# Elementwise products of the GLU tiles on VectorE instead of GpSimd, in a fixed order, and earlier loads before the first tile

## The chip, the cores and the metric

The kernel runs on one core of a Trainium2 chip. The metric is device time in microseconds from the first to the last instruction of that core. Three runs of the kernel before took 3117.59, 3122.15 and 3123.36 us; the median, 3122.15 us, is the time before. The profiled execution has a span of 3119.8 us and a mean granted TensorE clock of 0.989.

## The reference

One block of a conditioned transformer and its gradients, for 2048 rows of 512 features in bfloat16. Cut to what matters:

```
mod = (silu(c) @ w_mod) -> sa, ca, ga, sb, cb, gb          # six rows of 512
h   = layernorm(x) * (1 + ca) + sa
x1  = x + ga * A(h)            # recurrent attention, 64 segments of 32 rows, 8 memory rows
h2  = layernorm(x1) * (1 + cb) + sb
g, u = h2 @ w_gate, h2 @ w_up                             # 512 -> 1792
hh  = sigmoid(g) * u
out = x1 + gb * (hh @ w_down)                              # 1792 -> 512
```

The kernel returns `out` and the gradients of a given `grad_out` (called `dout`) with respect to x, the memory, the weights, c and w_mod. For the part that the change touches these are, per row: `db = dout * gb`, `du = (db @ w_down^T) * sigmoid(g)`, `dg = du * (u - hh)`, the gradient through the second layernorm `dx1`, then `da = dx1 * ga` and the product `dx1 * A(h)` that is summed over rows into the gradient of ga.

## The kernel before

The work runs in five stages, one after the other: the forward recurrence over 64 segments (`phase2`), the GLU with its forward and its backward (`phase3`, first part), the weight gradients of the GLU (second part), the backward recurrence (`phase4`) and the weight gradients of the attention (`phase5`). The change touches the last segment of `phase2` (the seam) and the first part of `phase3`.

**The GLU pipeline.** The 2048 rows are 16 tiles of 128. `run_pipeline` runs seven stages s0 to s6 over them: in iteration `it`, tile `it - k` is in stage k, and the deepest stage is written first. s0 makes `x1`, the layernorm and `h2`, and `db`. s1 sends `h2` and `db` through two transposing DMAs into `hdT`. s2 makes gate and up products (8 groups of four matmuls, 448 columns wide), ScalarE takes the sigmoid `sg` and copies `u`; then come `hh` and `umh = u - hh`. s3 makes four groups of matmuls `dp`, each turned into a piece of `du` by VectorE (L1077), then `dg`. s4 makes the output product, which ScalarE evacuates as `b_bf` (L1096), and leaves `t1` and `o_sb` for later. s5 makes the gradient product `hp`; VectorE works on it in the chain `dxh`, `pr_cb`, `junk`, `bb`, `cc`, `ta`, and with ScalarE's `tb` (L1140) makes `dx1`. s6 sums four products over the rows with matmuls onto `acc_ps` and transposes `da`.

**PSUM.** All products of s2 to s5 go through five buffers (`psM`, `mm()`), used in turn: 14 per iteration. A group of matmuls can start only when the product five places before it has been evacuated.

**Who does the elementwise work.** VectorE does most of it. GpSimd does five operations per tile: `rstd` (a power of 128x1), `db` (L1013), `umh` (L1054), `o_sb` (L1102) and `pr_ga` (L1152, `pr3` in the code). GpSimd's queue also issues the row stores to DRAM.

**Order.** `pin(i0, engines)` ties each instruction of an engine to the one before it in the program, so that the engine runs them in the order in which they are written. Where an engine is not pinned, the framework's scheduler picks the order when the kernel is built. In `phase3` TensorE and ScalarE are pinned up to iteration 2 only, and VectorE is not pinned. `late` is a list of small functions put off to the next `flush()`, of which there is one in s3 (between the `du` and `dg`) and one after each iteration.

**The seam.** `phase2` is pinned on all engines. In the last segment (s == 63) the weights and rows of the GLU are loaded into the space of `Wv`, `Wk` and `Wq`, the attention weights, as these are used for the last time. GpSimd's queue issues `w_gate`, `w_up`, `w_down` (1792 KB each, L819 to L821) after the segment's two Vst copies. The sync queue issues, in this order, the segment's k and q rows (`late_rows`), the rows of tile 0 (`glu_load`, L925 to L928) and the four modulation rows spread over 128 partitions (`mod_bc`, L366, 256 KB each). Then tile 1's rows follow, and the stores of the last segment. `norm` (L883) is the previous segment's GpSimd product, which is put off to the start of a segment.

Of the kernel before, what the change touches and what calls it, by code (L numbers as in the profile page):

```python
# [40 lines left out]
class K:  # L41
# [392 lines left out]
    def phase2(self):  # L434
# [13 lines left out]
        with ExitStack() as ctx:  # L448
# [232 lines left out]
            for s in range(NS):  # L681
# [10 lines left out]
                def proj(x, hf, eng):  # L692
                    pass_half(x, hf, lambda c: hT[:, c, :], RA[x], eng)
                    if hf == 1 and x != "v" and s < NS - 1:
                        rows_out(RA[x], DR[x], s, 1)
# [78 lines left out]
                        self.pair_mm(ps, [OT[:, off(h):off(h) + 32] for h in hs], [Wo[:, h, :] for h in hs], n, H // 2)  # L774
                    return ps

                if norms:
                    norms.pop()()
                proj("k", 0, "dve")
                proj("k", 1, "act")  # L780
                if s == 0:
                    for f in firsts["k"]:
                        f()
# [15 lines left out]
                if s + 1 < NS:  # L799
                    v_tails(s + 1)  # L800
                if s == NS - 1:
                    late_rows()
                    self.glu_first = {0: self.glu_load(0, nc.sync)}
                    for i in (2, 4, 3, 5):
                        self.mod_bc(None, i, "", t=self.bcs[i])
                st_exp(0)
                st_exp(1)
                vshift()
# [7 lines left out]
                if s < NS - 1:  # L816
                    nc.sync.dma_start(Pst[:], ET[:, :], transpose=True)
                else:
                    nc.gpsimd.dma_start(self.w_gate, io["B_w_gate"].rearrange("(c p) f -> p c f", p=128))  # L819
                    nc.gpsimd.dma_start(self.w_up, io["B_w_up"].rearrange("(c p) f -> p c f", p=128))  # L820
                    nc.gpsimd.dma_start(self.w_down, io["B_w_down"].rearrange("(fc p) d -> p fc d", p=128))  # L821
                den(1, or2)
# [108 lines left out]
    def phase3(self):  # L931
# [9 lines left out]
        with ExitStack() as ctx:  # L941
# [52 lines left out]
            def s0(j):  # L994
                r0, r1 = j * 128, (j + 1) * 128
                load(j + 1)
                st = ins.pop(j)
                a_rows = st["a_rows"]
                t0 = sbp.tile([128, D], F32, name="t0", tag="f32tmp", bufs=5)
                nc.vector.tensor_tensor(t0[:], a_rows[:], ga_bc[:], op=ALU.mult)  # L1000
                x1 = sbp.tile([128, D], F32, name="x1", bufs=4)
                nc.vector.tensor_tensor(x1[:], t0[:], st["x0"][:], op=ALU.add)
                sts = sbp.tile([128, 6], F32, name="st", bufs=2)
                nc.vector.bn_stats(sts[:], x1[:])
                mv = sbp.tile([128, 2], F32, name="mv", bufs=2)
# [5 lines left out]
                nc.gpsimd.tensor_tensor(rstd[:], ve[:], mhalf[:], op=ALU.pow)  # L1011
                db = sbp.tile([128, D], BF16, name="db", bufs=2)
                nc.gpsimd.tensor_tensor(db[:], st["dout"][:], gb_bc[:], op=ALU.mult)  # L1013
                self.pin(i0, [mybir.EngineType.Pool])
                nc.gpsimd.dma_start(self.DBROWS[r0:r1, :], db[:])
                xh2 = sbp.tile([128, D], BF16, name="xh2", bufs=5)
                xhf = sbp.tile([128, D], F32, name="xhf", tag="f32tmp", bufs=5)
                nc.vector.tensor_scalar(xhf[:], x1[:], mv[:, 0:1], rstd[:, 0:1], op0=ALU.subtract, op1=ALU.mult)
                nc.scalar.activation(xh2[:], xhf[:], AF.Copy)
                h2a = sbp.tile([128, D], F32, name="h2a", tag="f32tmp", bufs=5)  # L1020
                nc.vector.tensor_tensor(h2a[:], xhf[:], cb1_bc[:], op=ALU.mult)
                h2 = sbp.tile([128, D], BF16, name="h2", bufs=2)
                nc.vector.tensor_tensor(h2[:], h2a[:], sb_bc[:], op=ALU.add)
                nc.gpsimd.dma_start(self.H2ROWS[r0:r1, :], h2[:])
                st.update(db=db, x1=x1, rstd=rstd, xh2=xh2, h2=h2)
                return st

            def s1(j, st):
                hdT = sbp.tile([128, 2 * DC, 128], BF16, name="hdT", bufs=2)
                nc.sync.dma_start(hdT[:, 0:DC, :], st["h2"][:], transpose=True)  # L1030
                nc.sync.dma_start(hdT[:, DC:2 * DC, :], st["db"][:], transpose=True)
                st["hdT"] = hdT
                return st

            def s2(j, st):
                r0, r1 = j * 128, (j + 1) * 128
                hdT = st["hdT"]
                sg = sbp.tile([128, F], BF16, name="sg", bufs=2)
                u = sbp.tile([128, F], BF16, name="u", bufs=1)
                hh = sbp.tile([128, F], BF16, name="hh", bufs=2)  # L1040
                umh = sbp.tile([128, F], BF16, name="umh", bufs=1)
                for ch in range(NCH):
                    sl = slice(ch * CH, (ch + 1) * CH)
                    gp = mm()
                    for c in range(DC):
                        nc.tensor.matmul(gp[:, 0:CH], lhsT=hdT[:, c, :], rhs=w_gate[:, c, sl], start=(c == 0), stop=(c == DC - 1))
                    nc.scalar.activation(sg[:, sl], gp[:, 0:CH], AF.Sigmoid)
                    up = mm()
                    for c in range(DC):
                        nc.tensor.matmul(up[:, 0:CH], lhsT=hdT[:, c, :], rhs=w_up[:, c, sl], start=(c == 0), stop=(c == DC - 1))  # L1050
                    self.evac("act", u[:, sl], up[:, 0:CH])
                nc.vector.tensor_tensor(hh[:], sg[:], u[:], op=ALU.mult)
                nc.gpsimd.dma_start(self.HHROWS[r0:r1, :], hh[:])
                nc.gpsimd.tensor_tensor(umh[:], u[:], hh[:], op=ALU.subtract)  # L1054
                st.update(sg=sg, hh=hh, umh=umh)
                return st

            late = []

            def flush():  # L1060
                while late:
                    late.pop(0)()

            def s3(j, st):
                r0, r1 = j * 128, (j + 1) * 128
# [19 lines left out]
            def s4(j, st):  # L1085
                r0, r1 = j * 128, (j + 1) * 128
                hhT = st["hhT"]
                bp = mm()
                for fc in range(FC):
                    nc.tensor.matmul(bp[:], lhsT=hhT[:, fc, :], rhs=w_down[:, fc, :], start=(fc == 0), stop=(fc == FC - 1))  # L1090
                duT = sbp.tile([128, FC, 128], BF16, name="duT", bufs=1)
                dgT = sbp.tile([128, FC, 128], BF16, name="dgT", bufs=1)
                nc.sync.dma_start(duT[:], st["du"][:], transpose=True)
                nc.sync.dma_start(dgT[:], st["dg"][:], transpose=True)
                b_bf = sbp.tile([128, D], BF16, name="b_bf", bufs=2)
                nc.scalar.activation(b_bf[:], bp[:], AF.Copy)  # L1096

                def out():
                    t1 = sbp.tile([128, D], F32, name="t1", tag="f32tmp", bufs=5)
                    nc.vector.tensor_tensor(t1[:], b_bf[:], gb_bc[:], op=ALU.mult)  # L1100
                    o_sb = sbp.tile([128, D], BF16, name="o_sb", bufs=2)
                    nc.gpsimd.tensor_tensor(o_sb[:], t1[:], st["x1"][:], op=ALU.add)  # L1102
                    nc.gpsimd.dma_start(out_rows[r0:r1, :], o_sb[:])

                late.append(out)
                st.update(duT=duT, dgT=dgT, b_bf=b_bf)
                return st

            def s5(j, st):
# [36 lines left out]
                def out():  # L1146
                    nc.vector.tensor_tensor(da[:], dx1[:], ga_bc[:], op=ALU.mult)
                    nc.gpsimd.dma_start(self.DAROWS[r0:r1, :], da[:])

                late.append(out)  # L1150
                pr3 = sbp.tile([128, D], BF16, name="pr_ga", bufs=1)
                nc.gpsimd.tensor_tensor(pr3[:], dx1[:], a_rows[:], op=ALU.mult)  # L1152
                st.update(dh2b=dh2b, pr2=pr2, pr3=pr3, da=da, pr=pr)
                return st

# [52 lines left out]
            later = after  # L1208

            def after(it):  # L1210
                flush()
                later(it)

            self.run_pipeline(NT, [s0, s1, s2, s3, s4, s5, s6], deepest_first=True, after=after)
            self.pin_behind(i0, self.pinned, [ET.PE, ET.DVE, ET.Activation, ET.Pool, ET.SP])
            accs = self.flat(self.Wk, 2 * DC * F, 2 * D, F32)
            nc.vector.tensor_copy(accs[:], acc_ps[:, :])
# [910 lines left out]
```

The softmax here doesn't subtract the row's maximum and nothing guards it: scores larger than these inputs give would overflow.

## Time and profile before

| Stretch of the span, us | Stage | What TensorE does |
|---|---|---|
| 0 to 1000 | forward recurrence | busy, paced by itself |
| 1001.9 to 1008.9 | transposes of w_gate | slowed by ScalarE's evacuations |
| 1008.9 to 1023.9 | seam | idle, 15.0 us |
| 1023.9 to 1075.4 | first GLU iterations, with transposes of w_down and w_up | 48.6 of 51.5 us busy |
| 1075.4 to 1319.7 | 12 regular iterations of 20.42 us (one longer) | 229.3 of 244.3 us busy |
| 1319.7 to 1376 | last iterations, mixed with weight gradients | 50.0 of 56.4 us busy |
| 1376 to 3119.8 | weight gradients, backward recurrence | busy |

How to read it: the profile gives a busy time for each engine in any stretch, and for each instruction the idle time of its engine just ahead of it, with the work that ended that idle time. Where TensorE has the largest share, only idle time of TensorE can be won back; what the other engines wait for matters only if it makes TensorE wait later.

### The profile page before, as it was taken

The numbers are of one execution on the slowest core, as the hardware profiler recorded it, in microseconds if no ns is written. First come the engines' busy times: TensorE is split into PE (matmuls) and PEld (weight loads), VectorE is DVE, ScalarE is ACT, GpSimd is POOL, SyncE is SP. The second block draws the span as 40 slices with busy tenths as digits, with TensorE's granted clock in tenths as the row PEclk, the third lists the DMA queues.
The fourth block names the chain that finished last, engine by engine and source line by source line (L and its number), as shares of the span: only waits on it lengthen the run. The fifth ranks groups of instructions, "written<-read, shape, count | busy, mean of one in ns | idle before, by whom it ended". The sixth has DMA issues, their size and how long they took to land.

```text
span 3119.8 us, 106172 instructions
## 1 busy us (share of the span) xinstructions
PE 3005.8 (96%) x43845; PEld 1837.6 (59%) x43845; DVE 1644.2 (53%) x3735; ACT 1266.7 (41%) x3056; POOL 1502.8 (48%) x3022
## 2 busy tenths in 40 slices
PE   6999999999998899989989999999999999999999
PEld 3666666666665444445567777777777754455454
DVE  5556556656655789842255555555655542322321
ACT  2555555555554433322155555555555530110111
POOL 3667766767665566621244444444444422333321
PEclk8999999999999999999999999999999999999999
DMA  9887788788788789897589999999999998666674
GB/s 298 215 215 201 208 214 207 204 207 214 205 205 251 187 211 209 202 280 252 187 220 242 239 250 242 245 244 247 241 239 246 244 267 287 203 199 214 198 236 145
DMA packets 845944, 703.54 MB, mean 226 GB/s; under 512 B 544306, under 2 KB 717906, under 8 KB 845076
## 3 DMA queue, kind: packets, MB, share of 16 engines
q1 hardware_dynamic: 714148, 486.69, 61.7%
q0 software_dynamic: 60656, 148.64, 14.7%
q10 hardware_dynamic: 70656, 61.41, 6.3%
q8 instruction: 345, 5.65, 0.8%
q14 instruction: 139, 1.14, 0.1%
HBM read 294.93 MB, written 276.35 MB: 183 GB/s over the span
## 4 chain that ended last, share of the span: by engine, by line
PE 50%; issue 3%; DMA 3%; POOL 1%; DVE 0%; SPq 0%; ACT 0%; POOLq 0%; ACTq 0%; DVEq 0%
PE gps L1918 9%; PE dh_ps L215 8%; PE g_ps L1580 6%; PE pass_ps L255 5%; PE gps5o L1932 4%; PE dhq_ps L223 4%; PE gps L1267 3%; PE dh_tps L215 3%; PE dp_ps L1559 2%; PE tps L1492 2%; PE dp_ps L1567 1%; PE turn_ps L1446 1%; PE dh_ft L320 1%; POOL out_dram L1922 1%; PE wtp L1333 1%
## 5 line engine op out<-in xcount | busy, mean ns | idle before, releaser
L1918 PE MATMUL gps<-rows,hrows 128*128 128x512 bf16 (+2 forms) x2160 | 417.5, 356 | 0.0
L1918 PEld LDWEIGHTS <-hrows 128*128 128x128 bf16 x2160 | 211.0, 98 | 204.8
L255 PEld LDWEIGHTS <-hT 128*32 128x32 bf16 x6144 | 158.7, 97 | 160.9 <-issue 1.9
L1624 POOL COPY dOst<-RAd 96x512 bf16<-96x512 bf16 x128 | 75.6, 612 | 312.7 <-DVE RAd L63 312.2
L1922 POOL DMA_DIRECT2D out_dram<-ot x108 | 81.3, 753 | 247.6 <-DVE ot L63 140.3
L63 DVE CAST ot<-gps 128x512 bf16<-128x512 f32 (+3 forms) x76 | 48.1, 633 | 273.7 <-PE gps L1918 186.8
L61 ACT ACTIVATE ot<-gps 128x512 bf16<-128x512 f32 (+3 forms) x75 | 41.3, 551 | 352.3 <-PE gps L1918 232.9
L883 POOL TENSOR_TENSOR Pst<-Pst,rden 120x1408 bf16<-120x1408 bf16 x63 | 159.5, 2532 | 44.8 <-issue 28.6
L61 ACT ACTIVATE dVT<-g_ps 128x512 bf16<-128x512 f32 (+1 forms) x192 | 109.4, 570 | 95.6 <-PE g_ps L1580 95.0
L63 DVE CAST RA0v<-pass_ps 128x512 bf16<-128x512 f32 x128 | 88.5, 692 | 89.4 <-PE pass_ps L255 86.9
L215 PE MATMUL dh_ps<-WvT,dVT 128*32 128x512 bf16 x2048 | 133.3, 380 | 0.0
L255 PE MATMUL pass_ps<-Wv,hT 128*32 128x512 bf16 x2048 | 133.3, 380 | 0.0
L1932 PE MATMUL gps5o<-WoT,rows 128*128 128x512 bf16 x592 | 128.3, 379 | 2.1 <-DMA rows<-OSR 2.1
L255 PE MATMUL pass_ps<-Wk,hT 128*32 128x512 bf16 x2048 | 123.3, 383 | 1.5 <-ACT hT L873 1.1
L1569 DVE SCALAR_TENSOR_TENSOR dS<-dp_ps,Pst_l 128x512 bf16<-128x512 f32 (+1 forms) x192 | 112.1, 640 | 22.7 <-PE dp_ps L1567 22.7
L223 PE MATMUL at_ps<-Wo,OT 128*32 128x256 bf16 x4096 | 123.5, 273 | 0.1
L255 PE MATMUL pass_ps<-WoT,dyT 128*32 128x256 bf16 (+1 forms) x3072 | 122.4, 308 | 0.9 <-ACT dyT L1698 0.9
L223 PE MATMUL dhq_ps<-WqT,dQT 128*32 128x256 bf16 x4096 | 122.9, 273 | 0.0
L215 PE MATMUL dh_ps<-WkT,dKT 128*32 128x512 bf16 x2048 | 122.3, 381 | 0.0
L255 PE MATMUL pass_ps<-Wq,hT 128*32 128x512 bf16 x2048 | 121.6, 379 | 0.0
L223 PEld LDWEIGHTS <-dQT 128*32 128x32 bf16 x4096 | 109.9, 97 | 15.5
L717 ACT ACTIVATE ET<-st_ps 128x480 bf16<-128x480 f32 (+1 forms) x192 | 96.0, 535 | 42.6 <-ACT qT L61 34.7
(419 smaller groups left out, 7228.2 us busy)
## 6 DMA issues: line engine op xcount, KB each, us to landing
OSR<-Ost SPq DMA_DIRECT2D x64, 352.0 KB
OT<-OT SPq DMA_DIRECT2D x64, 352.0 KB
VT<-VTr SPq DMA_DIRECT2D x64, 352.0 KB
PS<-Pst SPq DMA_DIRECT2D x64, 352.0 KB
OT_l<-OT SPq DMA_DIRECT2D x64, 352.0 KB
Pst_l<-PS SPq DMA_DIRECT2D x64, 352.0 KB
VT_l<-VT SPq DMA_DIRECT2D x64, 352.0 KB
DVR<-rows_x POOLq DMA_DIRECT2D x64, 352.0 KB
```

Of the source, the lines that this page charges most:

```text
L61: return nc.scalar.activation(out, in_, AF.Copy)
L63: return nc.vector.tensor_copy(out, in_)
L215: self.nc.tensor.matmul(ps[32 * j:32 * j + 32, :], lhsT=lhsT, rhs=w, start=(n < 4), stop=(n >= total - 4), tile_position=(0, 32 * j))
L223: nc.tensor.matmul(ps[32 * j:32 * j + 32, :], lhsT=x[k], rhs=w[k][:, 256 * d:256 * d + 256], start=(n == 0), stop=(n == total - 1), tile_p ...
L255: self.nc.tensor.matmul(ps[32 * j:32 * j + 32, :], lhsT=lhs(c), rhs=rhs, start=(c == 0), stop=(c == DC - 1), tile_position=(0, 32 * j))
L717: nc.scalar.activation(part3(ET, pi)[:, 0:n, 0:120], st_ps[:, 0:n, 0:120], AF.Exp, scale=cfg.scale)
L883: nc.gpsimd.tensor_tensor(Pst[0:120, :, :], Pst[0:120, :, :], rden[:, :].unsqueeze(2).to_broadcast([120, G, 128]), op=ALU.mult)
L1569: nc.vector.scalar_tensor_tensor(out=part3(dS, pi), in0=ps[:, 0:n, :], scalar=cfg.scale, in1=part3(Pst, pi), op0=ALU.mult, op1=ALU.mult)
L1580: nc.tensor.matmul(ps[:, j, :], lhsT=lh[:, g * GW:(g + 1) * GW], rhs=rh[:, g * GW:(g + 1) * GW], start=True, stop=True)
L1918: nc.tensor.matmul(ps[:, 0:ng * E], lhsT=hrows[:, tp_, c * 128:(c + 1) * 128], rhs=rows[:, tp_, 0:ng * E], start=(tp_ == 0), stop=(tp_ == ...
L1922: nc.gpsimd.dma_start(outw[c * 128:(c + 1) * 128, h0:h0 + 3 * (ng - 1) + 1:3, :], ot[:, 0:ng * E].rearrange("p (h e) -> p h e", e=E))
L1932: nc.tensor.matmul(pss[gg][:], lhsT=src[0][:, src[1], gg * E:(gg + 1) * E], rhs=dyrows[:, tp_, :], start=(tp_ == order[0]), stop=(tp_ == o ...
```

## The change

The stated aim is to take the tile products off GpSimd, to give VectorE an order in which the pieces of `du` come first, and to have the loads ahead of the first tile issued sooner. It has six edits:

1. `db`, `umh`, `o_sb` and `pr_ga` move from GpSimd to VectorE. `rstd` and the DMA issues stay on GpSimd.
2. `db` is made after `h2` in s0, no longer before it.
3. `hh`, its store and `umh` are put off (`late`) to the flush after the iteration; `pr_ga` is put off together with `da`.
4. The flush after an iteration comes before the other work of that place from iteration 5 on, and after it (the weight transposes of iterations 2 to 4) before that.
5. VectorE is pinned to program order in the whole GLU pipeline.
6. In the last segment of the recurrence `w_gate` is issued right after the k projection and ahead of `norm`; the modulation rows come first on the sync queue, then tile 0's rows, then the k and q rows.

```diff
-                if norms:
+                if s < NS - 1 and norms:
                     norms.pop()()
                 proj("k", 0, "dve")
                 proj("k", 1, "act")
+                if s == NS - 1:
+                    nc.gpsimd.dma_start(self.w_gate, io["B_w_gate"].rearrange("(c p) f -> p c f", p=128))
+                    norms.pop()()
...
                 if s == NS - 1:
-                    late_rows()
-                    self.glu_first = {0: self.glu_load(0, nc.sync)}
                     for i in (2, 4, 3, 5):
                         self.mod_bc(None, i, "", t=self.bcs[i])
+                    self.glu_first = {0: self.glu_load(0, nc.sync)}
+                    late_rows()
...
-                    nc.gpsimd.dma_start(self.w_gate, io["B_w_gate"].rearrange("(c p) f -> p c f", p=128))
                     nc.gpsimd.dma_start(self.w_up, io["B_w_up"].rearrange("(c p) f -> p c f", p=128))
...
-                db = sbp.tile([128, D], BF16, name="db", bufs=2)
-                nc.gpsimd.tensor_tensor(db[:], st["dout"][:], gb_bc[:], op=ALU.mult)
                 self.pin(i0, [mybir.EngineType.Pool])
-                nc.gpsimd.dma_start(self.DBROWS[r0:r1, :], db[:])
...
                 nc.gpsimd.dma_start(self.H2ROWS[r0:r1, :], h2[:])
+                db = sbp.tile([128, D], BF16, name="db", bufs=2)
+                nc.vector.tensor_tensor(db[:], st["dout"][:], gb_bc[:], op=ALU.mult)
+                nc.gpsimd.dma_start(self.DBROWS[r0:r1, :], db[:])
...
-                nc.vector.tensor_tensor(hh[:], sg[:], u[:], op=ALU.mult)
-                nc.gpsimd.dma_start(self.HHROWS[r0:r1, :], hh[:])
-                nc.gpsimd.tensor_tensor(umh[:], u[:], hh[:], op=ALU.subtract)
+
+                def out():
+                    nc.vector.tensor_tensor(hh[:], sg[:], u[:], op=ALU.mult)
+                    nc.gpsimd.dma_start(self.HHROWS[r0:r1, :], hh[:])
+                    nc.vector.tensor_tensor(umh[:], u[:], hh[:], op=ALU.subtract)
+
+                late.append(out)
...
-                    nc.gpsimd.tensor_tensor(o_sb[:], t1[:], st["x1"][:], op=ALU.add)
+                    nc.vector.tensor_tensor(o_sb[:], t1[:], st["x1"][:], op=ALU.add)
...
                 def out():
                     nc.vector.tensor_tensor(da[:], dx1[:], ga_bc[:], op=ALU.mult)
                     nc.gpsimd.dma_start(self.DAROWS[r0:r1, :], da[:])
+                    nc.vector.tensor_tensor(pr3[:], dx1[:], a_rows[:], op=ALU.mult)
 
                 late.append(out)
                 pr3 = sbp.tile([128, D], BF16, name="pr_ga", bufs=1)
-                nc.gpsimd.tensor_tensor(pr3[:], dx1[:], a_rows[:], op=ALU.mult)
...
             def after(it):
+                if it < 5:
+                    later(it)
                 flush()
-                later(it)
+                if it >= 5:
+                    later(it)
 
             self.run_pipeline(NT, [s0, s1, s2, s3, s4, s5, s6], deepest_first=True, after=after)
+            self.pin(i0, [ET.DVE])
```

More of the change, by code (lines that the diff above doesn't have):

```diff
@@ L1033, in s1, with flush @@
                 return st
+            late = []
+            def flush():
+                while late:
+                    late.pop(0)()
             def s2(j, st):
@@ L1051, in s2 @@
                     self.evac("act", u[:, sl], up[:, 0:CH])
-                nc.vector.tensor_tensor(hh[:], sg[:], u[:], op=ALU.mult)
-                nc.gpsimd.dma_start(self.HHROWS[r0:r1, :], hh[:])
-                nc.gpsimd.tensor_tensor(umh[:], u[:], hh[:], op=ALU.subtract)
+                def out():
[3 more added lines that the diff above has]
+                late.append(out)
                 st.update(sg=sg, hh=hh, umh=umh)
                 return st
[L1058 to L1062, printed above, removed]
             def s3(j, st):
```

## The prediction

> **What bounds the kernel now.** I read the share of busy time first, then busy time by stretch, then TensorE's waits in the stretch that changes, then the instructions in order of time.
>
> ```profile
> PE 3005.8 (96%) x43845; PEld 1837.6 (59%) x43845; DVE 1644.2 (53%) x3735; ACT 1266.7 (41%) x3056; POOL 1502.8 (48%) x3022
> ```
>
> TensorE is idle for 114 us of 3119.8 in all, so no edit that leaves the matmuls alone can win more. By stretch (span; busy us of PE, PEld, DVE, ACT, POOL; clock; DMA share; GB/s):
>
> ```profile
> 1008.90:1023.90 15.00, 0.01 (x1) 0.00 (x0) 10.13 (x17) 2.44 (x4) 7.27 (x12) 0.58 0.70 228
> 1023.90:1075.40 51.50, 48.58 (x313) 26.51 (x314) 34.30 (x57) 24.57 (x39) 26.09 (x26) 0.96 0.80 181
> 1075.40:1319.65 244.25, 229.25 (x1177) 108.24 (x1176) 213.48 (x305) 86.55 (x155) 149.70 (x153) 1.00 0.88 208
> 1114.61:1135.03 20.42, 19.14 (x98) 9.00 (x98) 18.31 (x27) 7.25 (x13) 12.71 (x13) 1.00 0.91 202
> ```
>
> The third row is the 12 regular GLU iterations, with 15.0 us of TensorE idle; the fourth is one of them: 20.42 us, 19.14 of it TensorE, 18.31 VectorE. The seam (first row) loses another 15.0 us. TensorE's waits in the regular part (us in total, times, longest) make up those 15.0:
>
> ```profile
> PE mm L1050 <- DVE du L1077: 10.3, 11, 0.9
> PE mm L1046 <- ACT b_bf L1096: 4.7, 10, 1.7
> ```
>
> Both wait for a PSUM buffer. In order of time, one iteration shows why it comes late:
>
> ```profile
> 1108.77 3.58 POOL L1054 TENSOR_TENSOR umh<-u,hh 128x1792 bf16<-128x1792 bf16 x1
> 1110.12 2.80 DVE L1130 SCALAR_TENSOR_TENSOR junk<-dxh,xh 128x512 f32<-128x512 f32 x1
> 1113.99 0.58 ACT L1096 ACTIVATE b_bf<-mm 128x512 bf16<-128x512 f32 x1
> 1114.61 0.92 PE L1046 MATMUL mm<-Wk,hdT 128*128 128x448 bf16 x4 [0.34 <-ACT b_bf L1096]
> 1115.68 1.17 POOL L1152 TENSOR_TENSOR pr_ga<-dx,Wv 128x512 bf16<-128x512 f32 x1
> 1115.79 1.62 DVE L1147 TENSOR_TENSOR da<-dx,Wv 128x512 bf16<-128x512 f32 x1
> 1117.33 1.14 DVE L1077 TENSOR_TENSOR du<-mm,sg 128x448 bf16<-128x448 f32 x2
> 1118.00 0.92 PE L1050 MATMUL mm<-Wk,hdT 128*128 128x448 bf16 x4 [0.93 <-DVE du L1077]
> ```
>
> `junk` takes 2.80 us beside GpSimd's `umh` and ends about when it does; in iterations without that overlap it takes 0.68. It holds up `cc`, ScalarE's `tb`, then `b_bf` queued behind `tb`, and TensorE for 0.34. Then `da`, stretched to 1.62 by `pr_ga`, stands between the second and third `du` and costs TensorE 0.93.
>
> The seam:
>
> ```profile
> 1006.95 0.43 DVE L902 TENSOR_SCALAR Wv<-Wv 128x512 f32<-128x512 f32 x1 [3.24 <-DMA Wv<-MODROW]
> 1011.47 1.47 POOL L653 DMA_DIRECT2D AOA<-ao_b_rb  x3 [6.41 <-DMA Wv<-in_B_w_down_dram]
> 1013.13 0.57 POOL L1011 TENSOR_TENSOR rstd<-ve,mhalf 128x1 f32<-128x1 f32 x1
> 1021.34 1.23 SPq L1030 DMA_TRANSPOSE hdT<-h  x1
> 1023.93 1.67 PE L1046 MATMUL mm<-Wk,hdT 128*128 128x448 bf16 x4 [15.02 <-DMA hdT<-h]
> ```
>
> VectorE had `ve` for tile 0 at 1009.83. What ended last was GpSimd's queue: `rstd` stood behind AOA stores that waited for `w_down`. After that the sync queue was behind: `h2` was ready at 1017.04, its transpose issued at 1021.34.
>
> **What the Trainium skill says.** "SBUF — State Buffer", § Who interferes with whom: a VectorE instruction with two SBUF inputs and a GpSimd one that reads SBUF exclude each other; the later one blocks for the whole of the earlier. The trace agrees (`junk`, above). "GPSIMD Engine Reference", § 3.1: a two-input product takes GpSimd about twice as long as VectorE. Here 1.17 against 0.69 for f32 `pr_ga` and `da`, 3.58 against 1.08 in bf16. "VectorE: DVE Perf Modes", § The TRN2 errata: 691 ns for a float32 product of 512; rows here have 0.68 to 0.69. "DMA: Bandwidth & Descriptors", § Queues, rings and completion order: each DMA engine takes turns between the queues that have work. That fits the seam, where `w_down` and the modulation rows both took over 12 us; the trace doesn't show the turns.
>
> **Part 1: products moved (per tile).** VectorE's excess from blocking goes: `junk` 2.80 - 0.68 = 2.12; `t` L1000 1.75 - 0.69 = 1.06; `da` 1.62 - 0.69 = 0.93; `xhf` 1.38 beside `db`, where the like instruction at L1809 takes 0.54: 0.84. Together 4.95. Added: `db`, `o_sb`, `pr_ga` at 0.69 each (row of `t` L1100 and `da`) and `umh` at 1.08 (row of `hh`): 3.15. Net -1.8: VectorE's 18.31 becomes 16.5 of at best 19.14. GpSimd falls from 12.7 by 7.8 (1.15 + 3.58 + 1.87 + 1.17) and is out of the question.
>
> **Part 2: fixed order.** With no choice left, what counts is the loop of VectorE through one iteration, idle time included. From starts in the trace: the chain `dxh` to `dx1`, where unblocked (1070.17 to 1073.88), 3.7; four `du` 2.2; `da`, `pr_ga`, `t1`, `o_sb`, `dg` 3.6; s0 to `db` 6.1, with 0.7 waiting for `rstd`; `hh`, `umh` 2.1; `pr_gb` 0.4. Sum 18.1, under 19.14, so TensorE stays the bound with about 1 us to spare. Where the new waits lie: `dx1` waits for `tb` 0.28 as before, with the four `du` behind it and TensorE behind those. `hp` ends 6.2 us after s5's start, ScalarE's copy 6.84, the chain 10.6, the `du` 12.8. TensorE needs the first `du` out of its buffer at 12.9 and the fourth at 15.1, and `b_bf` (ready near 10.7) at 12.1. All have over 1 us. Both wait groups go: **-14 us** of 15.0; I leave 1 for the first of the 12, whose overlaps differ. `hh` and `umh` come later than now, but `u` (one buffer) isn't written again until 13 us into the next iteration and they are done at 6; `hhT` is used an iteration later. At no cost.
>
> **Part 3: first and last iterations.** In iterations 3 and 4 the evacuation of weight transposes now stands on VectorE behind all of s0 (6.1 us). Today TensorE waits 1.7 there once. I put +1 on each: **+2** (0 to 4). In iteration 18 `da` and `pr_ga` now follow four `du` (2.2 us), and TensorE, which already waits 0.86 for `pr_ga`, waits 1.2 more; up to 4.9 us of wait for HHROWS soon after can swallow it: **+0.6** (0 to 1.2).
>
> **Part 4: the seam.** `w_gate` waits for the last k product, about 982.6, against 988.6 now: 6 us sooner, with DMA engines 0.7 busy there. The three weights, 5.5 MB in 22.8 us, run at 241 GB/s; at some 150 in those 6 us, 0.9 MB is ahead, worth 3.7 us at `w_down`'s end and so at `rstd`. Behind the waiting issue on GpSimd stands `norm`, moved to about 983.5 and ending at 986.0, just ahead of the Vst copy at 986.10: nothing. Modulation rows go out 5 us sooner and drop off the chain; tile 0's rows come 2.5 us later, before the need at 1004. Then `xhf` is 0.8 shorter, and `h2` comes ahead of `db`, so its transpose needn't stand behind that of `db` (1.2). Sum 3.7 + 0.8 + 1.2 = 5.7: **-6**. Low end 2 (sync queue stays the last), high end 9 (its 4.3 us lag vanishes too).
>
> **Sum.** -14 + 2 + 0.6 - 6 = -17.4: 3122.15 - 17.4 = 3104.8, **3105 us**.
>
> **Rivals.**
> - *VectorE becomes the bound.* For it: only 1 us to spare, and dependent neighbours (`t1`, `o_sb`) start 0.73 apart rather than 0.61. Against: the sum already has these. A loop of 20.0 gives 0.4 x 12 = 5 instead of 14: 3114.
> - *The order itself stalls.* `rstd` behind GpSimd's DMA issues of 0.55 each, or `tb` behind evacuations on ScalarE, halts every later VectorE instruction. An extra 3 us makes the loop 21.0: +7 instead of -14: 3126, slower. Against: GpSimd's queue is two thirds empty after the change.
> - *DMA becomes the bound.* Its share is 0.91 of 20.42 = 18.6 us per tile; at 19.14 that is 0.97. Transposes have over 10 us between issue and use, so I expect a loss of a few us at most; with 0.5 per tile: 3111.
> - *The seam gives all.* 9 or more, ramp free: 3099.
>
> **Chances.** Main case 0.66 (3099 to 3111 with the ends of its terms), VectorE or DMA bound 0.16, nothing (seam and order both fail) 0.04, stall 0.06, seam gives all 0.08. The range 3098 to 3117 leaves out the stall, the nothing and tails. Faster than 3115.9: the main case, the last, and half of the second: 0.83; within 0.2%: 0.10; slower: 0.07.
>
> **What would show it.** Right: TensorE's waits for `du` and `b_bf` gone from the regular part, iterations of 19.2 us, `junk`, `t`, `da` at 0.69, first GLU matmul near 1018. Wrong: iterations above 19.5 with VectorE idle before `xhf` or `dx1` (order), VectorE without gaps (bound), TensorE waiting for `hdT`, `hhT` or `duT` (DMA), or `rstd` of tile 0 still after 1012 (seam).

## The result, and the profile after

The kernel after takes 3097.7 us (median of 4 runs, 3095.76 to 3099.95) against 3122.76 us for the kernel before in the same runs. The ratio is 0.9921 (95% interval 0.9904 to 0.9938): 25.1 us less, where 17.4 us less was predicted. The median lies 0.3 us below the fast end of the stated range, 3098 to 3117. The profiled execution has a span of 3093.9 us.

The busy times of the whole span:

```profile
PE 2997.4 (97%) x43769; PEld 1835.7 (59%) x43845; DVE 1628.3 (53%) x3799; ACT 1269.5 (41%) x3056; POOL 1378.6 (45%) x2958
```

VectorE took over four products per tile and is busy for 16 us less than before. TensorE is idle for 96.5 us of the span by its rows; before it was 114. (This trace holds 76 matmul records fewer than that of before, for the same matmuls, so its busy time is read slightly too low.) The same stretches as before (columns: span; busy us of PE, PEld, DVE, ACT, POOL; clock; DMA share; GB/s): seam, first iterations, regular part, one regular iteration:

```profile
1008.00:1019.57 11.57, 0.72 (x11) 0.43 (x8) 7.66 (x16) 3.37 (x5) 3.41 (x8) 0.64 0.68 205
1019.57:1070.67 51.10, 49.23 (x310) 26.66 (x313) 39.11 (x67) 24.78 (x39) 10.71 (x20) 0.95 0.80 187
1070.67:1295.50 224.83, 224.20 (x1161) 108.20 (x1172) 192.59 (x351) 89.02 (x155) 57.07 (x105) 1.00 0.97 225
1095.62:1114.43 18.81, 18.76 (x99) 9.03 (x99) 16.52 (x31) 7.47 (x13) 4.92 (x9) 1.00 0.94 227
```

In the regular part TensorE now has no gap worth a name (224.20 of 224.83 us), and twelve iterations run at 18.80 us each instead of 20.42. TensorE's two wait groups of before, for `du` and for `b_bf`, have no row any more. One iteration in order of time, with the instructions that were shown for before:

```profile
1100.68 1.09 DVE L1064 TENSOR_TENSOR umh<-u,hh 128x1792 bf16<-128x1792 bf16 x1
1104.28 0.68 DVE L1136 SCALAR_TENSOR_TENSOR junk<-dxh,xh 128x512 f32<-128x512 f32 x1
1106.04 0.57 ACT L1102 ACTIVATE b_bf<-mm 128x512 bf16<-128x512 f32 x1
1106.78 2.33 DVE L1083 TENSOR_TENSOR du<-mm,sg 128x448 bf16<-128x448 f32 x4
1108.28 0.92 PE L1054 MATMUL mm<-Wk,hdT 128*128 128x448 bf16 x4
1109.02 0.68 DVE L1153 TENSOR_TENSOR da<-dx,Wv 128x512 bf16<-128x512 f32 x1
```

`junk` is back at 0.68 us. The evacuation of `b_bf` ends at 1106.61, 1.67 us ahead of the matmuls that need its buffer; before, it ended at 1114.57, and the matmuls that had waited for it started 0.04 us later. All four `du` come ahead of `da`. The matmul line has no bracket: TensorE waited for nothing.

The seam in order of time:

```profile
1005.67 0.69 DVE L1002 TENSOR_TENSOR t<-Wv 128x512 f32<-128x512 bf16 x1 [1.54 <-DMA Wv<-AOA]
1007.26 1.47 POOL L653 DMA_DIRECT2D AOA<-ao_b_rb  x3 [4.57 <-DMA Wv<-in_B_w_down_dram]
1008.92 0.57 POOL L1013 TENSOR_TENSOR rstd<-ve,mhalf 128x1 f32<-128x1 f32 x1
1010.83 0.69 DVE L1022 TENSOR_TENSOR h<-h2a,Wv 128x512 bf16<-128x512 f32 x1
1017.09 1.21 SPq L1032 DMA_TRANSPOSE hdT<-h  x1
1019.57 0.93 PE L1054 MATMUL mm<-Wk,hdT 128*128 128x448 bf16 x2 [10.57 <-DVE db L1025]
```

GpSimd stands 4.57 us for `w_down` instead of 6.41, and `rstd` of tile 0 comes at 1008.92 instead of 1013.13. But `h` is ready at 1011.5 and its transpose is issued only at 1017.09: the sync queue issues stores of the last segment and the loads of later tiles in between. The bracket of the first matmul names a `db`, that of tile 1, which only ends at the same time: the matmul reads the transposed `h`, and it starts 2.48 us after the issue of that transpose, as before (2.59) and as with the sync queue fixed below (2.47).

### The profile page after: what moved, and what is told of

It is laid out like the page before. It is cut to its first block, busy times and chain, and to the rows that moved or that the text cites. A ratio compares the mean times of both kernels' runs of the same rounds, so it can differ in the third digit from the quotient of the medians.

```text
span 3093.9 us, 106049 instructions
## 1 busy us (share of the span) xinstructions
PE 2997.4 (97%) x43769; PEld 1835.7 (59%) x43845; DVE 1628.3 (53%) x3799; ACT 1269.5 (41%) x3056; POOL 1378.6 (45%) x2958
## 4 chain that ended last, share of the span: by engine, by line
PE 90%; DMA 4%; DVE 3%; issue 1%; POOL 1%; ACT 1%; SPq 0%; another core or an unknown queue 0%; DVEq 0%; POOLq 0%; ACTq 0%
PE pass_ps L255 18%; PE gps L1928 13%; PE dh_ps L215 8%; PE g_ps L1590 6%; PE gps5o L1942 4%; PE at_ps L223 4%; PE dhq_ps L223 4%; PE gps L1277 3%; PE mm L1121 3%; PE dh_tps L215 3%; PE turn_ps L264 2%; PE dp_ps L1569 2%; PE tps L1502 2%; PE tps L733 2%; PE mm L1081 2%; DVE RA0v L63 1%
## 5 line engine op out<-in xcount | busy, mean ns | idle before, releaser
L885 POOL TENSOR_TENSOR Pst<-Pst,rden 120x1408 bf16<-120x1408 bf16 x63 | 159.6, 2533 | 43.8 <-issue 28.4
```

The source lines that it names most:

```text
L885: nc.gpsimd.tensor_tensor(Pst[0:120, :, :], Pst[0:120, :, :], rden[:, :].unsqueeze(2).to_broadcast([120, G, 128]), op=ALU.mult)
```

## The experiments

Stages that no edit touches vary from one profiled execution to the next: the forward recurrence by up to 3.3 us, the part after the GLU mostly by 4.5. So I measure four distances from one mark, the last store of the attention's output rows by GpSimd (`AOA<-at_rb`, at 999.36 us before and 999.44 after). M is the start of the first GLU matmul. The "first iterations" run from M to the first sums of s6 (`acc_ps`), the regular part over the next twelve sums, the last iterations to the sixteenth. "All" is the mark to the sixteenth sum. Each of these distances comes from one profiled execution.

| Kernel | Median us | Ratio to before, 95% | M | First | Regular | Last | All |
|---|---|---|---|---|---|---|---|
| before | 3122.2 to 3123.7 | | 24.6 | 57.6 | 244.3 | 48.3 | 374.7 |
| after | 3097.7 | 0.9921 (0.9904 to 0.9938) | 20.1 | 57.3 | 225.7 | 46.4 | 349.4 |
| seam alone | 3125.4 | 1.0008 (1.0001 to 1.0014) | 21.4 | 63.1 | 244.3 | 47.8 | 376.6 |
| GLU edits alone | 3101.0 | 0.9933 (0.9918 to 0.9949) | 23.0 | 56.0 | 225.7 | 45.7 | 350.3 |
| moves alone | 3110.1 | 0.9963 (0.9949 to 0.9977) | 26.5 | 60.9 | 227.1 | 43.8 | 358.3 |
| order without moves | 3144.8 | 1.0070 (1.0055 to 1.0085) | 26.3 | 70.6 | 256.2 | 47.1 | 400.1 |
| after, umh on GpSimd | 3104.2 | 0.9938 (0.9922 to 0.9955) | 19.8 | 58.1 | 230.9 | 46.3 | 355.2 |
| after, three more products | 3111.7 | 0.9964 (0.9951 to 0.9977) | 20.0 | 61.7 | 235.0 | 45.8 | 362.5 |
| after, order not fixed | 3106.2 | 0.9944 (0.9929 to 0.9959) | 24.9 | 60.3 | 225.9 | 45.4 | 356.5 |
| after, sync queue fixed | 3096.5 | 0.9912 (0.9897 to 0.9926) | 16.1 | 57.9 | 225.7 | 45.0 | 344.5 |
| GLU edits, sync queue fixed | 3098.7 | 0.9923 (0.9909 to 0.9938) | 19.6 | 57.6 | 228.8 | 45.8 | 351.8 |
| sync fixed, w_down on ScalarE's queue | 3100.7 | 0.9931 (0.9914 to 0.9947) | 20.4 | 57.6 | 225.6 | 44.9 | 348.6 |
| umh alone | 3102.2 | 0.9936 (0.9921 to 0.9951) | 24.1 | 56.9 | 225.7 | 46.6 | 353.3 |
| umh and seam | 3099.4 | 0.9927 (0.9910 to 0.9943) | 20.9 | 57.0 | 225.7 | 47.4 | 350.9 |

The theory at the start was that of the prediction: the moves end the blocking, the fixed order takes `da` out from between the `du`, and the seam adds some microseconds. The rivals were that one of the parts does nothing, or costs.

### Seam alone

Edit 6 of the change, all else as before.

> The kernel before with the seam's edit alone (w_gate after the k projection, modulation rows first). Theory (blocking by GpSimd sets the regular part, GpSimd's queue behind w_down sets the seam): rstd of tile 0 near 1009 us instead of 1013, first GLU matmul near 1020 to 1021 instead of 1023.9, regular iterations unchanged at 20.42 us; 3119 us. Rival A (the seam's gain in the changed kernel came from db leaving the front of the first tile): first GLU matmul within 1 us of 1023.9; 3122 us.

3125.37 us, slower by 0.08%, where the theory said 3119. M came 3.2 us sooner from the mark. (In the profile's own time it is 1022.94, which would fit rival A, but there the recurrence ends 2.2 us later than in the profile of before.) The regular part is unchanged, as expected. But the first iterations took 63.05 us instead of 57.61. What happened there, in order of time:

```profile
1033.98 4.54 DVE L1025 TENSOR_TENSOR h<-h2a,Wv 128x512 bf16<-128x512 f32 x1
1034.38 3.58 POOL L1056 TENSOR_TENSOR umh<-u,hh 128x1792 bf16<-128x1792 bf16 x1
1038.44 0.61 DVE L63 COPY w_downT<-tp 128x896 bf16<-128x896 bf16 x1
1039.11 1.65 PE L981 MATMUL tp<-ident,Wv 128*128 128x128 bf16 x14 [3.63 <-DVE w_downT L63]
```

`h`, 0.69 us elsewhere, takes 4.54 beside GpSimd's `umh`; the copy of `w_downT` is queued behind it on VectorE, and TensorE waits 3.63 us for that copy's buffer. In the ten microseconds around this wait (1033 to 1043) the granted clock is 0.83, against 1.00 in the like stretch of before (1034 to 1044). So the head start was paid back by the very blocking that the GLU edits remove. The seam edits did not bring the two instructions together, though: in the kernel before they stand just as close (`h` at 1034.54, `umh` at 1034.94), but there `h` took 0.68 us and `umh` 3.72. Why the same meeting went the other way is open.

### GLU edits alone

The change without edit 6.

> The changed kernel with the seam as it was before. Theory: regular iterations 18.80 us, first GLU matmul near 1022 (xhf without db beside it), total near 3101 us. Rival A: the first GLU matmul is as early as in the changed kernel, 1019.6; total 3098 us.

3100.99 us, as the theory said. All twelve regular iterations are at 18.80 us; M comes 1.6 us sooner than before.

### Moves alone

The four products on VectorE, at their old places; no order fixed, nothing put off, old seam.

```diff
-                nc.gpsimd.tensor_tensor(db[:], st["dout"][:], gb_bc[:], op=ALU.mult)
+                nc.vector.tensor_tensor(db[:], st["dout"][:], gb_bc[:], op=ALU.mult)
... (umh, o_sb and pr3 likewise)
```

> The kernel before with the four products on VectorE where they stood, no fixed order, nothing put off, seam as before. Theory (blocking is the cause): junk, t, da at 0.69 us, TensorE's waits for du and b_bf gone, regular iterations 18.8 to 19.2 us, total 3101 to 3106 us. Rival B (the order is the cause, the moves only add 3.15 us to VectorE): iterations stay within 0.3 of 20.4 us, total near 3121 us.

3110.12 us, short of the 3101 to 3106 expected. The regular part is nearly that of after (227.1 us), so the theory held there. What is missing lies ahead of it: M is 1.9 us later than before, and the first iterations are 3.2 us longer.

### Order without moves

The kernel after with the four products put back on GpSimd: the order, the put-off pieces and the seam of after stay.

> The changed kernel, order and seam kept, with db, umh, o_sb and pr_ga on GpSimd again. Theory: the products block VectorE again; in a fixed order VectorE cannot go round them, its loop becomes the bound at 19.6 to 20.7 us per iteration; total 3108 to 3121 us. Rival B (order alone is enough): iterations near 18.8 us, total near 3098 us.

3144.83 us: slower than before, where 3108 to 3121 was expected. The twelve iterations took 18.8 to 25.5 us, 21.3 on average, where 19.6 to 20.7 was expected, and the first iterations took 70.6 us instead of 57.6, with TensorE waiting 11.7 us for VectorE's copies of `Wq`. In the regular part two things come together. The blocking is now fixed in place, and longer:

```profile
1169.42 3.59 POOL L1064 TENSOR_TENSOR umh<-u,hh 128x1792 bf16<-128x1792 bf16 x1
1170.03 3.53 DVE L1136 SCALAR_TENSOR_TENSOR junk<-dxh,xh 128x512 f32<-128x512 f32 x1
1175.27 1.44 PE L1054 MATMUL mm<-Wk,hdT 128*128 128x448 bf16 x4 [2.37 <-ACT b_bf L1102]
```

And on GpSimd, which isn't held to the written order throughout, `db` landed ahead of `rstd`, where it waits for a transposing DMA to release its buffer:

```profile
1163.85 1.16 POOL L1025 TENSOR_TENSOR db<-Wk,Wv 128x512 bf16<-128x512 bf16 x1 [4.20 <-DMA hdT<-db]
1164.97 0.56 POOL L1013 TENSOR_TENSOR rstd<-ve,mhalf 128x1 f32<-128x1 f32 x1
1165.57 0.55 DVE L1017 TENSOR_SCALAR xhf<-x,mv,rstd 128x512 f32<-128x512 f32 x1 [4.48 <-POOL rstd L1013]
```

With its order fixed, VectorE can do nothing else meanwhile. This is the prediction's second rival (the order itself stalls); it happened in this kernel and not in after, where `db` is no longer on GpSimd. How the loss splits between the two was not measured.

### After with umh on GpSimd

```diff
-                    nc.vector.tensor_tensor(umh[:], u[:], hh[:], op=ALU.subtract)
+                    nc.gpsimd.tensor_tensor(umh[:], u[:], hh[:], op=ALU.subtract)
```

> The kernel after with one edit: umh = u - hh (128 x 1792) goes back from VectorE (1.09 us) to GpSimd (3.59 us in the kernel with all products on GpSimd); the fixed VectorE order, the other three products on VectorE and the seam edits stay. In that other kernel VectorE's junk, which stood beside umh, took 3.53 us instead of 0.68, and the next block of TensorE waited for what came behind it. Theory (the gain of the regular part hangs on keeping the 3.6 us stretch away from VectorE's path, with umh the largest piece of it): VectorE's loop of about 17.85 us loses 1.09 of its own work and gains up to 3.0 us of standing still, 19.8 us an iteration against TensorE's 18.80, so twelve iterations lengthen by about 12 us: about 3110 us, and an instruction of VectorE beside umh shows 3 us or more. Rival (what counts is VectorE's own work and the other three products; one product on GpSimd fits into the 0.95 us that VectorE is idle plus the 1.09 us it gives up): iterations stay at 18.80 us, 3097 us.

3104.18 us, between the theory and the rival, and 19.5 us less than before. Most iterations are 19.29 us (18.80 to 20.6). TensorE's wait for `du` is 1.6 us, in one iteration, where it was 10.3 us in eleven before; its wait for `b_bf` is 2.2 us in seven. An iteration of 19.29:

```profile
1239.46 3.59 POOL L1064 TENSOR_TENSOR umh<-u,hh 128x1792 bf16<-128x1792 bf16 x1
1239.62 0.69 DVE L1130 SCALAR_TENSOR_TENSOR dxh<-mm,Wv 128x512 f32<-128x512 f32 x1 [0.67 <-ACT dh2b L1127]
1240.23 0.69 DVE L1133 TENSOR_TENSOR pr_cb<-mm,xh 128x512 bf16<-128x512 f32 x1
1240.84 2.77 DVE L1136 SCALAR_TENSOR_TENSOR junk<-dxh,xh 128x512 f32<-128x512 f32 x1
1245.31 0.92 PE L1054 MATMUL mm<-Wk,hdT 128*128 128x448 bf16 x4 [0.31 <-ACT b_bf L1102]
```

The block has its old shape: `junk` takes 2.09 us more than in after. What VectorE saves by not computing `umh` lies ahead of its wait for `dh2b` and doesn't shorten the chain behind that wait, from `dxh` over `tb` to `b_bf`. In after this chain ended at 1106.61 (`b_bf`), 1.67 us ahead of the matmuls that need the buffer; 2.09 uses that up and 0.42 more, and the iteration grew by 0.49. The expectation put up to 3.0 us on the block: it left out that two instructions ahead of `junk`, `dxh` and `pr_cb`, run at 0.69 beside `umh`. Each has one input in PSUM (`mm`). "SBUF — State Buffer", § Who interferes with whom, has this: a VectorE instruction with at most one SBUF input, outside the two-port modes, doesn't contend with GpSimd. The trace agrees.

### After with three more products

```diff
+                for _ in range(3):
+                    xtra = sbp.tile([128, D], BF16, name="xtra", bufs=1)
+                    nc.vector.tensor_tensor(xtra[:], st["dout"][:], gb_bc[:], op=ALU.mult)
```

They stand behind `db` in s0.

> The kernel after with three more VectorE products of 128 x 512 in each tile (0.69 us each for f32 operands, 0.42 to 0.69 for bf16; they are additional work, copies of db into a scratch tile, that nobody reads), emitted directly behind db. This measures the spare time of VectorE in the regular part. Theory (VectorE is busy or in its loop for about 17.85 us of the 18.80 of an iteration, so about 0.95 us is spare): 3 x 0.42 to 3 x 0.69 = 1.3 to 2.1 us more make an iteration 19.1 to 19.9 us, twelve of them add 4 to 13 us: 3102 to 3111 us. Rival (VectorE has far more spare than its idle rows show, since waits at dxh, xhf and dx absorb it): iterations stay 18.80, time 3098 us within 1 us.

3111.7 us, at the upper end of the theory; ten of the twelve iterations take 19.69 us, give or take 0.01.

```profile
1185.18 2.13 DVE L1029 TENSOR_TENSOR xtra<-Wk,Wv 128x512 bf16<-128x512 bf16 x3
```

The three start at 1185.18, and `hh` behind them starts at 1187.24, while `hh` follows `db` as closely in after as these do: they add 2.06 us to VectorE's loop, which now has no idle time before `dxh` left. The iteration grows by 0.89, so 2.06 - 0.89 = 1.17 us was spare, and VectorE's loop in after is 18.80 - 1.17 = 17.63 us.

### After without the fixed order

```diff
-            self.pin(i0, [ET.DVE])
```

> The kernel after with only the fixing of VectorE's order left out: the four products stay on VectorE, the written order and the seam edits stay, but the tile scheduler places VectorE's instructions. Theory (the regular part needs only the moves, since the kernel with the moves alone also ran most iterations at 18.80 us; the fixed order pays in the seam and in the first iterations, where the moves alone came 7.1 us later): iterations of 18.80 us with one or two longer, first iterations some microseconds longer, 3100 to 3108 us. Rival A (the fixed order is worth nothing, only the late pieces and seam edits are): 3098 us. Rival B (without it du falls behind da again in each iteration): up to 2 us x 12, 3120 us.

3106.23 us. Eleven iterations are 18.80 us and one is 19.10: the regular part doesn't need the order. The seam does. In order of time on VectorE:

```profile
1008.69 0.69 DVE L1002 TENSOR_TENSOR t<-Wv 128x512 f32<-128x512 bf16 x1 [1.82 <-DMA Wv<-AOA]
1016.64 0.69 DVE L1025 TENSOR_TENSOR db<-Wv 128x512 bf16<-128x512 bf16 x1 [7.26 <-DMA Wv<-AOA]
1020.29 0.55 DVE L1017 TENSOR_SCALAR xhf<-x,mv,rstd 128x512 f32<-128x512 f32 x1 [0.75 <-POOL rstd L1013]
1022.58 0.69 DVE L1022 TENSOR_TENSOR h<-h2a,Wv 128x512 bf16<-128x512 f32 x1
```

The scheduler put `db`, which needs a load that lands at 1016.6, and the work of tiles 1 and 2 ahead of `xhf` and `h` of tile 0. VectorE stands 7.26 us with tile 0's normalization behind it, and M is 4.8 us later than in after. The first iterations are 3.0 us longer; in them TensorE waits 6.2 us for VectorE's copies of transposed weights, against 0.3 in after. The moves alone have the same order (`db` ahead of tile 0's sum) and lose in the same places.

### After with the sync queue fixed

```diff
+                if it == 5:
+                    self.pin(i0, [ET.SP])
```

In `after` of the pipeline: the sync queue keeps the written order through the first iterations.

> The kernel after with the order of the sync queue fixed as written through the first iterations of the GLU, so that the two transposes of hdT of tile 0 stand ahead of the loads of tiles 2 to 6 on that queue (in the kernel after they stood behind them: h of tile 0 was ready at about 1011.5 us and its transpose was issued at 1017.09). Theory (the sync queue is what ends last in the seam now): the transpose is issued at about 1011.6, the one of db behind it at about 1014, the first matmul of the GLU starts near 1014 to 1016 instead of 1019.57, and the whole kernel is 3 to 5 us shorter, about 3093 us. Rival (the seam's head start is given back: the loads that come later hold up the norms of tiles 1 to 4 and the first iterations): the first matmul is earlier, the seventh iteration is not, 3097 to 3100 us.

3096.5 us (3094.72 to 3097.61). In time this is between the theory (about 3093) and the rival (3097 to 3100). By the marks the theory held: M is 4.1 us sooner and all of it stays (344.5 against 349.4). The two medians can't be told apart, as their ranges overlap. Two other things now end last:

```profile
1009.67 0.50 POOL L653 DMA_DIRECT2D AOA<-ao_b_rb  x1 [4.20 <-DMA Wv<-in_B_w_down_dram]
1015.80 1.20 SPq L1032 DMA_TRANSPOSE hdT<-h  x1
1018.27 1.30 PE L1054 MATMUL mm<-Wk,hdT 128*128 128x448 bf16 x3 [7.65 <-DMA hdT<-h]
```

`w_down` holds GpSimd again (its mark is at 1002.22), and the transpose still comes 1.9 us after `h` ends at 1013.93. The profile puts 2.6 us of the sync queue's wait ahead of it to the landing of the `VT` store, which that queue had issued at 1012.63; why a transpose waits for that store is not shown.

### GLU edits with the sync queue fixed

As the last, with the old seam.

> The kernel with the GLU edits of after, the seam of before (gate weight and modulation rows loaded late, the rows of tile 0 after the late rows) and the sync queue fixed as written through the first iterations. It tells whether the seam edits are worth something once the scheduler no longer places the transposes behind later loads. Theory (the head start of the seam edits was lost on the sync queue): without the seam edits this stays 2 to 5 us behind the same kernel with them (3096.5), 3098 to 3101 us, its first GLU matmul near 1021 to 1024. Rival (the seam edits are worth nothing at the end): 3096 us within 1 us.

3098.65 us, in the range of the theory; M is 3.5 us later than with the seam edits. In this one profile two regular iterations also are longer, with 2.5 us of TensorE waiting for `hhT`, a transposing DMA.

### Sync queue fixed, w_down on ScalarE's queue

```diff
-                    nc.gpsimd.dma_start(self.w_down, io["B_w_down"].rearrange("(fc p) d -> p fc d", p=128))
+                    nc.scalar.dma_start(self.w_down, io["B_w_down"].rearrange("(fc p) d -> p fc d", p=128))
```

> The kernel after with the sync queue fixed as written through the first iterations, and the load of w_down issued on ScalarE's queue instead of GpSimd's. In the kernel with only the sync queue fixed, GpSimd stood 4.20 us at the store of AOA until w_down had landed (1009.67), and rstd of tile 0 came 1.4 us after its operand was ready; db waited until 1015.84 for a load of the sync queue. Theory (the landing of w_down holds GpSimd, and rstd with it): that wait is gone, rstd starts at about 1010 instead of 1011.33, the first matmul of the GLU at about 1017 instead of 1018.27; at the end 1 us or less of it is left, about 3095.5 us. Rival A (the AOA store waits for another transfer of the same time, or db's operand ends last anyway): no change, 3096.5. Rival B (ScalarE stands behind the load's own waits in the attention's last stage): later by microseconds.

3100.71 us: 4.2 us slower than with the sync queue alone fixed, as rival B has it, but not for its reason. GpSimd's wait for `w_down` is gone, as expected, but the sync queue took 17.01 us to issue the four loads of attention rows for tile 0 (4.05 with `w_down` on GpSimd's queue), and M is 4.4 us later. The profile puts 13.1 of the 17.01 us to the landing of `w_down`: the wait for it moved from GpSimd's queue to the sync queue. Why a queue that did not issue `w_down` waits for it stays open; the run shows that removing the visible wait was not enough.

### umh alone

The kernel before with one word changed:

```diff
-                nc.gpsimd.tensor_tensor(umh[:], u[:], hh[:], op=ALU.subtract)
+                nc.vector.tensor_tensor(umh[:], u[:], hh[:], op=ALU.subtract)
```

> The kernel before with one edit: umh = u - hh is computed by VectorE (1.09 us) instead of GpSimd (3.58); the other three products stay on GpSimd, the order stays with the tile scheduler, the seam stays. Theory (in the kernel before, junk stood 2.1 us beside umh, and tb, b_bf, dx and du were queued behind it; da's stretch of 0.94 beside pr_ga only reached TensorE because VectorE was late): junk falls to 0.68, dx ends about 2 us earlier, the waits for b_bf (0.34) and du (0.94) both go, iterations fall from 20.42 to 18.8 to 19.1 us, about 13 to 18 us in all: 3105 to 3111 us. Rival (da ahead of the last two du is a cost of its own, so du first and the other products are needed): only the b_bf wait goes, 0.3 to 0.5 us an iteration, 3117 to 3120 us.

3102.15 us: 20.4 of the 25.1 us, and 21.5 of 25.3 by the marks. That is below the 3105 to 3111 of the theory. All twelve iterations are 18.80 us. One of them:

```profile
1199.84 1.09 DVE L1054 TENSOR_TENSOR umh<-u,hh 128x1792 bf16<-128x1792 bf16 x1
1201.30 0.69 DVE L1124 SCALAR_TENSOR_TENSOR dxh<-mm,Wv 128x512 f32<-128x512 f32 x1 [0.37 <-ACT dh2b L1121]
1202.52 0.68 DVE L1130 SCALAR_TENSOR_TENSOR junk<-dxh,xh 128x512 f32<-128x512 f32 x1
1205.95 1.17 POOL L1152 TENSOR_TENSOR pr_ga<-dx,Wv 128x512 bf16<-128x512 f32 x1
1206.08 1.60 DVE L1147 TENSOR_TENSOR da<-dx,Wv 128x512 bf16<-128x512 f32 x1
1207.60 1.14 DVE L1077 TENSOR_TENSOR du<-mm,sg 128x448 bf16<-128x448 f32 x2
1208.79 0.92 PE L1050 MATMUL mm<-Wk,hdT 128*128 128x448 bf16 x4
```

`da` still stands between the second and third `du`, and is still stretched to 1.60 by `pr_ga`. Yet TensorE waits for nothing, because the whole chain runs some 2 us sooner against TensorE's work. And `umh` on VectorE costs little: it fills part of the time for which VectorE waited for `dh2b` anyway (0.98 in the iteration shown for before, 0.37 here).

### umh and seam

The edit of `umh` alone, together with edit 6.

> The kernel before with the seam edits (gate weight and modulation rows sooner) and umh on VectorE; the other products stay on GpSimd and no order is fixed. With the seam edits alone the first matmul of the GLU came at 1022.94 and the seventh iteration's sums at 1085.99 (63.05 us later, 5.4 more than before), where VectorE's h of a later tile took 4.54 us beside umh and a copy of w_downT, which TensorE waited 3.6 us for, was queued behind it. Theory (that loss was umh blocking VectorE, not the seam edits themselves): no h above 1.5 us, the stretch from the first matmul to the seventh iteration is 57 to 58 us, iterations run at 18.80, and with a first matmul near 1023 the time is 3099 to 3102 us. Rival (the sooner loads displace later ones, and the first iterations wait for them whatever umh does): 62 to 63 us again, 3105 to 3107 us.

3099.36 us, as the theory said. The first iterations take 56.97 us, not 63.05, and the group of `h` in them, in the groups by line (busy us, mean ns):

```profile
L1025 DVE TENSOR_TENSOR h<-h2a,Wv 128x512 bf16<-128x512 f32 x4 | 2.7, 687 | 0.1
```

So it was `umh` that ate the gain of the seam alone. With these two edits the time can't be told from that of after.

## Why the prediction was right, and where it wasn't

The direction and the place of the gain held. The kernel is 7 us faster than forecast, just past the fast end of the range. The prediction's fast cases had their surplus in the seam and the first iterations; it came in the regular part. By the marks the terms compare so:

| Step | Forecast | Measured |
|---|---|---|
| Parts 1 and 2, regular part | -14 | -18.6 |
| Part 3, first iterations | +2 | -0.4 |
| Part 3, last iterations | +0.6 | -1.9 |
| Part 4, M | -6 | -4.4 |
| Sum | -17.4 | -25.3 |

**Part 1 held to the tenth.** `junk`, `da` and `t` are at 0.68 us, `xhf` at 0.55, and VectorE is busy for 16.52 us of an iteration where 16.5 was worked out.

**Part 2: the mis-sized term is the floor.** The sum took TensorE's busy time, 19.14 us, as the shortest iteration, so it counted 15.0 us of waits as all that could be won. The floor is 18.80, and the regular part became 18.6 us shorter. The reason is in the rows: where nothing waits, groups of four matmuls start 0.75 to 0.76 us apart (1108.28 and 1109.04 in after), but each row lasts 0.92 us, with an end that the profile models. A wait counted from the end of a row therefore misses about 0.16 us. The two gaps of an iteration of before held 0.34 us more than their rows said (20.42 - 18.80 = 1.62, rows 0.34 + 0.94). Over the eleven iterations with waits that makes 18.6 - 15.0 = 3.6 of the 4.6 us missed; the other 1.0 was left for the first iteration and wasn't needed. "Perfetto Trace Analysis", § Identifying the Most-Contended Engine, warns that a matmul busy share is no good measure of the distance to the limit, as matmuls are pipelined; here it put the floor 0.34 us too high. The number was in the trace: the last of the regular iterations of before, without a wait, took 18.81 us. For the same reason idle time by the rows, the 114 us of the whole span or the 15.0 us here, is not the most that can be won. VectorE's loop was forecast at 18.1 with 1 us to spare; the three added products measured 17.63 and 1.17, so the rival "VectorE becomes the bound" was as near as said and didn't come.

**Part 2 also gave each wait a cause of its own.** It gave the wait for `du` to `da` standing between the pieces, and its removal to the fixed order. `umh` alone removed it, with `da` in its old place and stretched. But all the other edits without that one nearly removed it too (10.3 to 1.6 us), with `junk` still blocked. So, as far as these runs tell, the wait needed both: VectorE late by `junk`, and `da`, stretched, in between. The gains don't add up: in the regular part `umh` alone is worth 18.6 us, everything but `umh` 13.3, and all together 18.6. Once `umh` is moved, the other three moves and the order add nothing there. Which of them helps while it is not was not separated.

**What the fixed order is for.** With the products moved, it pays in the seam and first iterations: without it after loses 8.5 us (3106.2 against 3097.7), of which the marks show 4.8 at M, where `db` with a late operand goes ahead of tile 0's normalization, and 3.0 in the first iterations. The prediction had this only as "`h2` comes ahead of `db`".

**Part 3 had the wrong sign.** It put the evacuations of weight transposes behind all of s0 and added 1 us to each of two iterations. TensorE's wait for `Wq` on VectorE, 1.7 us before, is gone; waits of the transposes are 1.6 us in all, against 2.9. In the last iterations the scheduler placed the sums behind the first eleven matmuls of `duT`, so the wait for `pr_ga` that was to grow is gone.

**Part 4 was right in mechanism, short in sum.** `rstd` came 4.2 us sooner (3.7 forecast), and VectorE's wait for the modulation rows went. Tile 0's rows were to land before the need and did not: `t` waited 1.54 us for them. That cost nothing, since `ve` was there at 1008.21 and GpSimd came to `rstd` only at 1008.92. `h` was ready 5.5 us sooner, but its transpose lagged it by 5.6 us instead of 4.3: 1.3 us were lost on the sync queue, the case named for the low end; fixing that queue gave 4.1 us back at M. Four pairs of kernels with and without the seam edits give 3.2 (before), 2.8 (GLU edits), 3.5 (sync fixed) and 3.2 us (umh alone) at M. Whether it is kept depends on what follows: alone it ended at +1.9 us.

DMA, the third rival, is at a share of 0.97 in the regular part of after, and TensorE never waits for it there. It is close: with the old seam and the sync queue fixed, TensorE waited 2.5 us for `hhT` in that part.

One sum of the chances is off by a little: the main case, the last and half of the second make 0.82, not 0.83.

## What to carry to other kernels

Where a trace shows one stretched VectorE instruction beside a long GpSimd product, move that product first and measure it alone: one of four gave four fifths of the gain here, and the waits further down the same chain went with it. Measure the rest without it too: all the other edits together gave 19.5 us, nearly as much, so such shares can't be added. Take the floor of a pipelined stage from an iteration that waited for nothing, not from TensorE's busy time. Before an in-order engine, ask of each instruction when its operands land: a fixed order is worth something where loads are still arriving, and it turns one late operand into a stop for all behind it.

## What was not expected of the hardware

- A load sooner can cost more than it brings: M was 3.2 us sooner with the seam alone, and the end of the GLU 1.9 us later, since `h` was blocked beside `umh` (4.54 us instead of 0.69).
- An instruction of VectorE blocked by `umh` ends about 0.56 us after it in each case shown (1173.56 against 1173.01; 1243.61 against 1243.05; `h` 1038.52 against 1037.96), so it does nearly all its work (0.68 to 0.69 us alone) after `umh`. That `h` was blocked although its row begins 0.40 us ahead of that of `umh`. In the kernel before, with the same 0.40 us between the rows, `h` took 0.68 us and `umh` 3.72, 0.13 more than its median. GpSimd's spans are rough, so which of them really came first is open in both.
- GpSimd's bf16 difference of 1792 columns takes 3.3 times what VectorE takes (3.59 and 1.09), while for 512 columns with float32 inputs the ratio is 1.7 (`pr_ga`, 1.17 and 0.69).
